# The last weight pieces cut into 100 and 28 rows, and the small loads moved to GpSimd's queue, in a decode step of window attention with a gated MLP

## The chip, the cores and the metric

The kernel runs on one core of one Trainium2 chip. The metric is the device time of one launch in microseconds (us), the median of several runs; lower is better.

## The reference, cut to what matters

```python
def reference(A_x, A_k_cache, A_v_cache, A_wq, A_wo, B_x, B_w_in, B_w_sp, B_b_sp, B_w_out):
    x = A_x                                   # (2, 1, 512): batch 2, one new position
    xn = _layernorm(x, axis=-1)
    # attention over the last 4096 of 32768 cached positions; 32 query heads, 8 kv heads, Dh 128
    q = (xn @ wq)                             # wq (512, 4096)
    scores = einsum("bhqd,bhkd->bhqk", q, k) * Dh ** -0.5
    s = (softmax(scores) @ v) @ wo            # wo (4096, 512)
    # gated MLP
    z = gelu(xn @ w_in)                       # w_in (512, 1792)
    z1, z2 = z[..., :896], layernorm(z[..., 896:])
    y = (z1 * (w_sp * z2 + b_sp)) @ w_out     # w_sp (1, 1), b_sp (1,), w_out (896, 512)
    return x + s * silu(y)
```

Everything is float32. The windows of the two caches are 33.6 MB each, the four weight matrices together some 22 MB, and all of it is read once. The small inputs are `x` (4 KB) and the two scalars `w_sp` and `b_sp`.

## The kernel before

All large loads go through SyncE's DMA queue, in the order in which the program lists them: `win`, `wout`, two halves of `wq`, then the key and value tiles of the eight kv heads, and at last `wo`. Each is one DMA of 128 partition rows. The large tiles except `wout` rotate through a ring of four slots (`slot`, `RING = 4`); a load waits on SyncE until the slot's last reader is done. A cache tile has 4 MB, 32 KB for each of 128 rows.

The work on the engines is one stream per engine, kept in program order by the wrapper `InOrder` (`pe`, `dve`, `act`, `sp`). GpSimd is called directly (`nc.gpsimd`): its memsets, the making of `ident`, and one DMA.

The small loads are the copy of `x` for the layer norm (`xs`, 2 rows of 2 KB, line 91), the scalars `w_sp` and `b_sp` (`wb1`, lines 105 and 106), all three issued by ScalarE, and a second copy of `x` laid out for the final sum (`x4`, line 110), issued by GpSimd. `xs` starts a chain on VectorE (`st`, `mv`, `va`, `rs`, `xn`) that ends in `xnT`, which the first product (`z`, lines 219 to 225) multiplies with `win`. `wb1` is used by one small matmul (`wb_ps`) after it. Then come the queries (`queries(0)` to `queries(3)`), which need `wq`.

For each kv head VectorE turns the key tile (`turn`), TensorE multiplies it with the queries (`scores`), a softmax follows, and TensorE multiplies with the value tile (`values`).

The end, lines 493 to 549, is where most of the change sits. The rows of `wo` belong to three sets of kv heads, `SETS = ((0, 4, 16), (4, 2, 8), (6, 2, 8))`: heads 0 to 3 with 16 columns j, heads 4 and 5 with 8, heads 6 and 7 with 8. They are loaded in pieces, all on 128 rows, a piece of n columns having n * 2 KB in each row. Before the change there are eight pieces: 8 and 8 columns (set 0), 4 and 4 (set 1), and 4, 2, 1 and 1 (set 2). In set 2 they arrive last and in this order. `blocks` lists the pieces. `wo_early(n)` multiplies piece n into the bank `part`; four groups of 32 PSUM rows take turns, and `EARLY = 24` columns, sets 0 and 1, go there. ScalarE copies `part` to `parts`, four matmuls with `rowm` add up its groups into `so`, and the pieces of set 2 are multiplied into `so` directly, four matmuls to a column. VectorE then multiplies `so` with `gate`, adds `x4`, and ScalarE's queue stores the result.

Of the kernel before, what the change touches and what calls it, by code (L numbers as in the profile page):

```python
# [14 lines left out]
P = 128  # L15
# [27 lines left out]
def kernel(  # L43
# [13 lines left out]
    nc = tc.nc  # L57
    pe, dve, act, sp = (InOrder(tc, e) for e in (nc.tensor, nc.vector, nc.scalar, nc.sync))
# [24 lines left out]
    def slot(name, *shape):  # L83
        return ring.tile([P, *shape], F32, tag="slot", name=name)
# [3 lines left out]


    xs = sb.tile([B, D], F32, tag="p", name="xs", bufs=1)  # L90
    act.dma_start(xs, x[:, 0, :])
    win_v = w_in.rearrange("(p k) f -> p k f", p=P)
    win = slot("win", KT, F)
    sp.dma_start(win, win_v)
# [4 lines left out]
    for a in range(0, KT, 2):  # L99
        t = slot(f"wq{a}", 2, HQ * DH)  # L100
# [1 line left out]
        wqt += [t[:, 0], t[:, 1]]  # L102

    wb1 = cst.tile([1, 2], F32, tag="wb1", name="wb1")
    act.dma_start(wb1[:, 0:1], bass.AP(tensor=w_sp.tensor, offset=w_sp.offset, ap=[[1, 1], [1, 1]]))
    act.dma_start(wb1[:, 1:2], bass.AP(tensor=b_sp.tensor, offset=b_sp.offset, ap=[[1, 1], [1, 1]]))
    x4 = cst.tile([P, DC], F32, tag="x4", name="x4")
    nc.gpsimd.memset(x4, 0.0)
    by_group = [[DC, G], [D, B], [1, DC]]
# [351 lines left out]
    def spread_after(p):  # L461
        if p is not None and p.n in ends:
            spread(ends[p.n])
# [26 lines left out]
        scores(cur, 0, 1, 2, 3)  # L490


    wo_s = []
    for kv, n, nj in SETS:
        r0, r1 = kv * REP * DH, (kv + n) * REP * DH
        wo_s.append(wo[r0:r1, :].rearrange("(p j) d -> p j d", j=nj))
    blocks = []
    for first, of in ((0, (0,)), (1, (1, 2))):
        t = slot(f"wo{first}", 16, D)
        a = 0  # L500
        for i in of:
            nj = SETS[i][2]
            for j, n in (((0, 8), (8, 8)), ((0, 4), (4, 4)), ((0, 4), (4, 2), (6, 1), (7, 1)))[i]:
                sp.dma_start(t[:, a : a + n, :], wo_s[i][:, j : j + n, :])
                blocks.append((t[:, a : a + n, :], sets[f"oT{i}"][1], j))
                a += n
    EARLY = 24
# [2 lines left out]
    def wo_early(n):  # L510
        nonlocal done
        t, oT, j = blocks[n]
        for a in range(t.shape[1]):
            g = done % G
            pe.matmul(
                part[32 * g : 32 * g + 32, :], oT[:, j + a, :], t[:, a, :], start=(done < G), stop=(done >= EARLY - G)
            )
            done += 1
# [9 lines left out]
    wo_early(0)  # L528
    gathered(units[-1])
    spread_after(units[-1])  # L530
    for n in range(1, 4):
        wo_early(n)
    parts = sb.tile([P, D], F32, tag="o", name="parts", bufs=1)
    act.activation(parts, part, AF.Copy)
    so = bank("so", DC)
    for g in range(G):
        pe.matmul(so[32 * g : 32 * g + 32, :], rowm, parts[:, g * DC : (g + 1) * DC], start=True, stop=False)
    for n in range(4, len(blocks)):
        t, oT, j = blocks[n]
        for a in range(t.shape[1]):  # L540
            for g in range(G):
                pe.matmul(
                    so[32 * g : 32 * g + 32, :], oT[:, j + a, :], t[:, a, g * DC : (g + 1) * DC],
                    start=False, stop=(j + a == oT.shape[1] - 1),
                )
# [32 lines left out]
```

## Time and profile before

| what | value |
|---|---|
| median of 3 runs | 218.35 us (218.16 to 218.53) |
| the profiled execution | 218.31 us |
| its span, first to last instruction | 216.1 us |
| read from HBM | 89.40 MB, 414 GB/s over the span |
| busy: TensorE, VectorE, ScalarE, GpSimd | 135.0, 104.9, 24.0, 4.0 us |

The profiled execution is 2.2 us longer than its span; that is what lies before the first and behind the last instruction. "Busy" is the time in which an engine executes; none of the four is busy for the whole span. The DMA engines, of which the core has 16, are listed apart, as a share of the 16 that is busy in each stretch of the span. A DMA queue's row gives packets: a transfer of 128 rows has one packet a row and a few small ones that report its end.

### The profile page before, as it was taken

Reading aid. Unit: us, or ns where it says so; the run is one execution under the profiler, and the core shown is the slowest. Engines: PE = TensorE matmul, PEld = TensorE weight load, DVE = VectorE, ACT = ScalarE, POOL = GpSimd, SP = SyncE. Lnnn points to the kernel's source line nnn. Section 1 sums busy time; section 2 is a strip of 40 time slices with the busy share of each in tenths; the row PEclk is TensorE's granted clock in tenths of the full one; section 3 lists DMA queues with packets and bytes.
Section 4 is the critical chain, followed back from the end, with each engine's and each line's share of the span. In section 5 each row is a group of like instructions: output and inputs, shape, how many; then the busy total and the mean of one; then the engine's idle time right before and its main releaser. Section 6 shows DMA issues by size and latency. Waiting matters only on the chain.

```text
span 216.1 us, 2106 instructions
## 1 busy us (share of the span) xinstructions
PE 135.0 (62%) x862; PEld 42.8 (20%) x862; DVE 104.9 (49%) x161; ACT 24.0 (11%) x60; POOL 4.0 (2%) x20
## 2 busy tenths in 40 slices
PE   0173294627774993973594199179567489968653
PEld 0120021113111221320131023033111122342221
DVE  2604014439539539658508910885784684511201
ACT  4103003200001021101021002012000012031010
POOL 7000000000000000000000000000000000000000
PEclk9998569995588598796589559959966969999998
DMA  7999999999999999999999999999999999999990
GB/s 255 425 437 455 418 455 418 429 431 418 455 400 461 403 455 418 443 425 425 443 421 443 406 449 425 449 425 428 437 418 449 400 456 409 443 409 417 417 373 25
DMA packets 4092, 89.52 MB, mean 414 GB/s; under 512 B 486, under 2 KB 498, under 8 KB 884
## 3 DMA queue, kind: packets, MB, share of 16 engines
q1 hardware_dynamic: 4032, 89.39, 96.7%
q8 instruction: 6, 0.10, 0.2%
q14 instruction: 2, 0.02, 0.0%
q10 hardware_dynamic: 20, 0.01, 0.0%
q0 software_dynamic: 32, 0.00, 0.0%
HBM read 89.40 MB, written 0.00 MB: 414 GB/s over the span
## 4 chain that ended last, share of the span: by engine, by line
DMA 71%; PE 13%; DVE 12%; SPq 1%; ACT 1%; issue 1%; ACTq 0%; DVEq 0%
DMA v<-in_A_v_cache_dram 42%; DMA k<-in_A_k_cache_dram 20%; DMA wo<-in_A_wo_dram 9%; DVE kt L37 8%; PE acc L37 7%; PE s L37 3%; PE pp L37 2%; SPq L37 1%; ACT p L37 1%; DVE pT L37 1%; DVE sm L37 1%; DVE qw L37 1%; DVE both L37 0%; PE col L37 0%; DVE res L37 0%
## 5 line engine op out<-in xcount | busy, mean ns | idle before, releaser
L37 DVE STREAM_TRANSPOSE kt<-k 128x2048 f32<-128x2048 f32 x32 | 72.5, 2286 | 3.5 <-DMA k<-in_A_k_cache_dram 3.5
L37 PE MATMUL acc<-v,pT 128*32 128x512 f32 x256 | 40.1, 781 | 11.4 <-DMA v<-in_A_v_cache_dram 10.5
L37 PE MATMUL s<-kt,qw 128*32 128x512 f32 x256 | 39.8, 669 | 4.6 <-DVE kt L37 4.1
L37 PE MATMUL pp<-p,swap 128*128 128x512 f32 x16 | 12.4, 871 | 21.3 <-ACT p L37 21.3
L37 DVE CUSTOM_DVE_ANT_1 sm<-s,own 128x512 f32<-128x512 f32 x8 | 5.5, 692 | 34.2 <-PE s L37 34.2
L37 PEld LDWEIGHTS acc<-v,pT 128*32 128x32 f32 x256 | 10.5, 152 | 39.4 <-issue 35.6
L37 PE MATMUL q_ps<-wq,xnT 128*32 128x512 f32 x64 | 9.7, 732 | 11.0 <-DMA wq<-in_A_wq_dram 11.0
L37 ACT ACTIVATE o<-acc,diag 128x128 f32<-128x128 f32 x30 | 8.7, 369 | 69.3 <-PE acc L37 68.9
L37 PEld LDWEIGHTS s<-kt,qw 128*32 128x32 f32 x256 | 9.5, 120 | 34.0 <-issue 20.8
L37 ACT ACTIVATE p<-sm,nb 128x512 f32<-128x512 f32 x8 | 5.8, 725 | 70.8 <-DVE nb L37 70.8
L37 DVE TENSOR_TENSOR lsum<-pl,diag 128x4 f32<-128x4 f32 x3 | 0.5, 162 | 16.7 <-PE pl L37 16.7
L37 DVE STREAM_TRANSPOSE pT<-pp 128x512 f32<-128x512 f32 x8 | 5.7, 714 | 5.7 <-PE pp L37 5.6
L37 PE MATMUL z<-win,xnT 128*32 128x448 f32 x32 | 5.7, 887 | 3.9 <-DMA win<-in_B_w_in_dram 3.9
L37 PE MATMUL part<-wo,oT 128*32 128x512 f32 x48 | 6.0, 600 | 2.8 <-DMA wo<-in_A_wo_dram 2.8
L37 PE MATMUL col<-o,selw 128*32 128x128 f32 (+1 forms) x28 | 7.6, 436 | 0.0
L37 PEld LDWEIGHTS pp<-p,swap 128*128 128x128 f32 x16 | 2.8, 218 | 22.0 <-ACT p L37 22.0
L37 PE MATMUL mo<-mg,same 128*128 128x16 f32 x16 | 3.2, 273 | 5.8 <-DVE mg L37 5.3
L37 DVE TENSOR_TENSOR res<-so,gate 128x128 f32<-128x128 f32 x1 | 0.3, 292 | 10.4 <-PE so L37 10.4
L37 ACT ACT_TABLE_LOAD x4 | 5.1, 1283 | 2.0 <-issue 1.9
L37 PE MATMUL xnT_ps<-ident,xn 2*128 2x2 f32 x4 | 0.6, 252 | 7.5 <-DVE xn L37 7.5
L37 PE MATMUL qj_ps<-qT,selj 128*128 128x64 f32 x8 | 2.0, 428 | 4.9 <-DVE qT L37 4.9
L37 PEld LDWEIGHTS q_ps<-wq,xnT 128*32 128x32 f32 x64 | 2.0, 126 | 14.6 <-DMA wq<-in_A_wq_dram 11.1
(110 smaller groups left out, 65.0 us busy)
## 6 DMA issues: line engine op xcount, KB each, us to landing
k<-in_A_k_cache_dram SPq DMA_DIRECT2D x8, 4096.0 KB, 23.4
v<-in_A_v_cache_dram SPq DMA_DIRECT2D x8, 4096.0 KB, 31.2
wq<-in_A_wq_dram SPq DMA_DIRECT2D x2, 4096.0 KB, 28.9
wo<-in_A_wo_dram SPq DMA_DIRECT2D x2, 2048.0 KB
win<-in_B_w_in_dram SPq DMA_DIRECT2D x1, 3584.0 KB, 11.1
wo<-in_A_wo_dram SPq DMA_DIRECT2D x3, 1024.0 KB, 23.2
wout<-in_B_w_out_dram SPq DMA_DIRECT2D x1, 1792.0 KB, 15.0
wo<-in_A_wo_dram SPq DMA_DIRECT2D x1, 512.0 KB, 26.9
```

Of the source, the lines that this page charges most:

```text
L37: return self.tc.keep_in_program_order(call(*args, **kwargs))
```

## The change

Three edits. `xs`, `w_sp` and `b_sp` are issued on GpSimd's queue instead of ScalarE's, ahead of `x4`. The second piece of set 1, 4 columns, becomes two pieces of 2 columns; the loop over `wo_early` goes one piece further for it, so that the same 24 columns go into `part`. And each of the last two pieces of set 2, 1 column each (256 KB), is loaded by two DMAs, one for rows 0 to 99 and one for rows 100 to 127. The matmuls are the same in number and shape.

```diff
-    act.dma_start(xs, x[:, 0, :])
+    nc.gpsimd.dma_start(xs, x[:, 0, :])
...
-    act.dma_start(wb1[:, 0:1], bass.AP(tensor=w_sp.tensor, offset=w_sp.offset, ap=[[1, 1], [1, 1]]))
-    act.dma_start(wb1[:, 1:2], bass.AP(tensor=b_sp.tensor, offset=b_sp.offset, ap=[[1, 1], [1, 1]]))
+    nc.gpsimd.dma_start(wb1[:, 0:1], bass.AP(tensor=w_sp.tensor, offset=w_sp.offset, ap=[[1, 1], [1, 1]]))
+    nc.gpsimd.dma_start(wb1[:, 1:2], bass.AP(tensor=b_sp.tensor, offset=b_sp.offset, ap=[[1, 1], [1, 1]]))
...
+    LATE = ((2, 6), (2, 7))
...
-            for j, n in (((0, 8), (8, 8)), ((0, 4), (4, 4)), ((0, 4), (4, 2), (6, 1), (7, 1)))[i]:
-                sp.dma_start(t[:, a : a + n, :], wo_s[i][:, j : j + n, :])
+            for j, n in (((0, 8), (8, 8)), ((0, 4), (4, 2), (6, 2)), ((0, 4), (4, 2), (6, 1), (7, 1)))[i]:
+                deal = ((0, 100), (100, P)) if (i, j) in LATE else ((0, P),)
+                for p0, p1 in deal:
+                    sp.dma_start(t[p0:p1, a : a + n, :], wo_s[i][p0:p1, j : j + n, :])
                 blocks.append((t[:, a : a + n, :], sets[f"oT{i}"][1], j))
                 a += n
...
-    for n in range(1, 4):
+    for n in range(1, 5):
         wo_early(n)
...
-    for n in range(4, len(blocks)):
+    for n in range(5, len(blocks)):
```

## The prediction, made before the changed kernel ran

> **What bounds the kernel now.** I read the page's slices first, then its DMA queues, then the chain that ended last, and last the timeline and the windows of the final stretch.
>
> ```profile
> DMA  7999999999999999999999999999999999999990
> q1 hardware_dynamic: 4032, 89.39, 96.7%
> q8 instruction: 6, 0.10, 0.2%
> q14 instruction: 2, 0.02, 0.0%
> q10 hardware_dynamic: 20, 0.01, 0.0%
> q0 software_dynamic: 32, 0.00, 0.0%
> DMA 71%; PE 13%; DVE 12%; SPq 1%; ACT 1%; issue 1%; ACTq 0%; DVEq 0%
> ```
>
> The DMA engines are at 90% or more in every slice but the first and the last. So the waits of the middle cost nothing as long as the queue stays fed, and time can be lost or won only where the transfers start, where they end, or if fewer than 16 engines work. The end is told by the chain of waits:
>
> ```profile
> 164.31 28.21 DMA v<-in_A_v_cache_dram
> 192.53 19.79 DMA wo<-in_A_wo_dram
> 212.33 0.04 issue
> 212.37 0.47 PE so L37 x8
> ```
>
> The kernel ends with the last piece of wo, which lands at 192.53 + 19.79 = 212.32; then come only eight matmul instructions, two VectorE operations and the store. The timeline shows the pieces ahead of it, each waited for in its turn:
>
> ```profile
> 207.33 1.06 PE L37 MATMUL part<-wo,oT 128*32 128x512 f32 x8 [1.43 <-DMA wo<-in_A_wo_dram]
> 208.46 0.60 ACT L37 ACTIVATE parts<-part 128x512 f32<-128x512 f32 x1 [10.35 <-PE part L37]
> 209.11 0.43 PE L37 MATMUL so<-parts,rowm 128*32 128x128 f32 x8 [0.72 <-ACT parts L37]
> 209.91 2.25 PE L37 MATMUL so<-wo,oT 128*32 128x128 f32 x56 [0.38 <-DMA wo<-in_A_wo_dram]
> 211.07 0.38 PEld L37 LDWEIGHTS so<-wo,oT 128*32 128x32 f32 x16 [0.35 <-DMA wo<-in_A_wo_dram]
> 211.73 0.16 PEld L37 LDWEIGHTS so<-wo,oT 128*32 128x32 f32 x8 [0.28 <-DMA wo<-in_A_wo_dram]
> 212.37 0.43 PE L37 MATMUL so<-wo,oT 128*32 128x128 f32 x8 [0.21 <-DMA wo<-in_A_wo_dram]
> ```
>
> Set 2's four pieces start at 209.91, 211.07, 211.73 and 212.37. One column (256 KB) thus takes 212.37 - 211.73 = 0.64 us. Now the windows of the last stretch; the last two columns are the busy share of the 16 DMA engines and GB/s:
>
> ```profile
> 209.70:209.90 0.20, 0.00 (x0) 0.02 (x1) 0.00 (x0) 0.00 (x0) 0.00 (x0) 1.00 0.94 358
> 209.90:210.10 0.20, 0.18 (x8) 0.20 (x12) 0.00 (x0) 0.00 (x0) 0.00 (x0) 1.00 0.68 266
> 210.10:210.30 0.20, 0.20 (x16) 0.20 (x12) 0.00 (x0) 0.00 (x0) 0.00 (x0) 1.00 0.57 215
> 210.70:210.90 0.20, 0.20 (x12) 0.03 (x3) 0.00 (x0) 0.00 (x0) 0.00 (x0) 1.00 0.55 205
> 210.90:211.10 0.20, 0.12 (x8) 0.03 (x4) 0.00 (x0) 0.00 (x0) 0.00 (x0) 1.00 0.41 154
> 211.10:211.30 0.20, 0.20 (x8) 0.20 (x12) 0.00 (x0) 0.00 (x0) 0.00 (x0) 1.00 0.43 164
> 211.30:211.50 0.20, 0.20 (x16) 0.15 (x8) 0.00 (x0) 0.00 (x0) 0.00 (x0) 1.00 0.30 113
> 211.50:211.70 0.20, 0.20 (x9) 0.00 (x0) 0.00 (x0) 0.00 (x0) 0.00 (x0) 1.00 0.14 51
> 211.70:211.90 0.20, 0.18 (x11) 0.16 (x8) 0.00 (x0) 0.00 (x0) 0.00 (x0) 1.00 0.03 10
> ```
>
> This is the view that decides. The 16 engines do not finish together. About half of them have nothing left from 210.1 on (0.57 of 16 is 9, and 205 GB/s is half of what all of them moved). Of the rest two stop near 210.95, and six, one after the other, between 211.1 and 211.8. Every large transfer gives each engine the same 8 rows (4032 packets are 28 transfers of 128 rows and 16 reports), so the late half must have lost time to something else. The queues offer it: six packets of 0.10 MB together, some 16 KB each, and two smaller ones, all of instructions. Eight fetches, eight late engines: I take it that each fetch held up one engine and that nothing later makes it up.
>
> **The last two pieces, 100 and 28 rows.** What matters is how the rows are dealt. The 20 packets of q10 are the four small transfers of ScalarE's queue: 2 + 1 + 1 + 8 rows are 12, so 8 report an end, where a transfer of 128 rows has 16 reports. That fits equal shares on as many engines as the first dimension allows: 2 for xs, 1 for each scalar, 4 for the store, which is laid out as 4 by 2. By equal shares 100 rows go to ten engines, 10 rows each, and 28 rows to fourteen, 2 rows each. If both start at the same end of the numbering, then for each of the two pieces ten engines carry 12 rows instead of 8, four carry 2, and two carry none. A row costs 0.64 / 8 = 0.08 us on its engine. Over both pieces that is +8 rows, +0.64 us, for ten engines; -12 rows, -0.96 us, for four; -16 rows, -1.28 us, for two.
>
> [...]
>
> The end is then set by the last engine of the ten. No view says which numbers the late engines have. If the very last one, done at about 211.8, is among the ten, the end comes 0.64 us later. That is the value that I take: ten places of sixteen hold it if nothing is known, and for a gain all six of the latest would have to be the six spared ones. Bounds: below, -0.2 us, worked out with the first rival; above, +1.0 us, if the ten engines, writing blocks of ten rows at once, get in each other's way by a quarter of their 24 rows (24 x 0.08 = 1.92 us, a quarter is 0.5, half of it hidden by the earlier ends of the others). The matmuls of these pieces each wait for two transfers instead of one; behind them on TensorE is only the next piece.
>
> **The second piece of set 1 in two.** The piece of 4 columns is worked on at 207.33; the copy and the fold of part are over at 209.11 + 0.43 = 209.54, and only at 209.91, after 0.38 us of waiting for data, does the next product start. An earlier half would be done earlier and wait longer: no gain. Its price is one more packet a row. Set 2's piece of 2 columns took 211.73 - 211.07 = 0.66 to the next start and 1.16 from the one before; twice 1.25 for two such pieces against the 2.49 us between the starts of 4-column pieces (204.84 to 207.33) is 0.01 us. I take 0.02, between 0 and 0.05. If the cover of 0.38 us were gone, the fold would start set 2's products late, yet these have another 0.1 to 0.3 us of slack at each piece.
>
> ```profile
> 204.84 1.06 PE L37 MATMUL part<-wo,oT 128*32 128x512 f32 x8 [0.56 <-DMA wo<-in_A_wo_dram]
> 180.67 12.20 SPq L37 DMA_DIRECT2D wo<-in_A_wo_dram  x8
> ```
>
> SyncE has three more DMAs to issue (one here, two for the cut pieces). The eight of now took 12.20 us with their waits for the slot, so three more take 4.6 us at the most; the last was issued at 192.53 and landed 19.79 us later, and that lead covers them. Nothing is queued behind them on SyncE but the end; without the lead, their issue would stand in full ahead of the last landing.
>
> **The small loads on GpSimd.**
>
> ```profile
> 0.75 0.56 ACTq L37 DMA_DIRECT2D xs<-in_A_x_dram  x1
> 1.30 0.68 POOL L110 DMA_DIRECT2D x<-in_A_x_dram  x1 [0.21 <-POOL ident masks.py:197]
> x<-in_A_x_dram POOLq DMA_DIRECT2D x1, 4.0 KB, 6.5
> 3.28 0.68 DVE L37 BATCH_NORM_STATS2 st<-xs 2x6 f32<-2x512 f32 x1 [0.50 <-DMA xs<-in_A_x_dram]
> 8.24 0.17 DVE L37 COPY xnT<-xnT_ps 128x8 f32<-128x8 f32 x1 [0.87 <-PE xnT_ps L37]
> 11.99 5.70 PE L37 MATMUL z<-win,xnT 128*32 128x448 f32 x32 [3.86 <-DMA win<-in_B_w_in_dram]
> PE q_ps L37 <- DMA wq<-in_A_wq_dram: 11.0, 2, 7.9
> ```
>
> Now xs is there at 3.28. On GpSimd's queue it takes what x takes, 0.68 us of issue and 6.5 us to land, at worst until about 8, at best as quickly as now. From st to the end of xnT are 8.41 - 3.28 = 5.1 us, so xnT comes between 8.4 and 13.1, and z, which waits for win until 11.99, starts 0 to 1.1 us late. This is covered: the first queries wait up to 7.9 us for wq afterwards. If that cover were gone, it would cost the 1.1 us. SyncE's load of the second key tile waits for z's slot, and with a queue in which a landing comes 19.79 or 28.21 us after its issue (the two of the chain above), 1 us later is nothing. GpSimd's own work behind the three issues, the making of ident and the memsets, comes some 3 x 0.68 = 2 us later; rowm (VectorE) waits for ident, and st behind it waits for xs longer than that. The scalars are needed only after z. ScalarE is rid of issuing, 0.56 us for xs, that nobody waited for. I take 0, between -0.1 (two engines start the large transfers without xs in between) and +0.1 (more small packets on all engines).
>
> **Sum.** Against the profiled execution's 218.31: +0.64 + 0.02 + 0 gives 218.97; the median of the runs is 0.04 above this execution, so 219.0 us. The measurement of this kernel tells about 0.2% (0.44 us) from no change.
>
> **Rivals.** First, not slower: the six latest engines are exactly the six spared ones. For it speaks the count, six of six, with a shift (0.64 + 0.96 or 1.28) about as large as their lag of some 1.2 to 1.7 us behind the half that is done at 209.9 to 210.1; against it, that nothing ties them to these numbers. The two engines done near 210.95 must then be among the ten, and end at 210.95 + 0.64 = 211.6 instead of 211.8: -0.2 us, 218.15 with the rest. TensorE would allow it: the 2-column piece still lands for 211.07, its 16 weight loads took 0.38 us, those of the two last pieces would take as long, and all is over well before 212.84, where it is now. This decides from the point where no engine done after 211.1 is among the ten; one at 211.2 would make it a draw.
>
> Second: the shares are not equal, the rows are dealt over all 16 engines as evenly as they go (7 and 2). Then an engine has at most 9 rows for 8 in each piece, and the end is 2 x 0.08 = 0.16 us later: 218.5. Against it speak the 20 packets of q10. [...]
>
> Third: the last engine is among the spared ones but a middle one of the six is not. The end is then 0.64 us behind 211.3 to 211.6, so at 211.94 to 212.24 where it is now 211.8: 218.5 to 218.8.
>
> **How the numbers follow.** My forecast gets 0.47, with its own range of 218.8 to 219.3; the first rival 0.33, the second 0.08, the third 0.12. Slower by over 0.2%: 0.47 and a little of the third, less the forecast's own lower edge, 0.48. Faster by over 0.2% needs 0.44 us, twice what the first rival gives; 0.09 for a fetch that moves or a start that gains more than I see. The rest, 0.43, is within 0.2%. The range of 217.9 to 219.3 takes in the first rival with its spread and the forecast.
>
> **What would show it.** The page's q1 row would count 27 x 144 + 2 x (128 + 10 + 14) = 4192 packets by equal shares, 4208 if every transfer used 16. In the timeline the last two starts would be near 212.1 and 213.0 instead of 211.73 and 212.37, 0.8 to 0.96 us apart, while the pieces before them keep their times. The windows would show a share near 0.6 until the end instead of a fall in steps. st would start later than 3.28, z up to 1.1 us later, and the first queries when they do now. I am wrong if the last piece lands before 212.3, or if the large transfers themselves end the stretch before wo at another time.

## The result, and the profile after

The changed kernel takes 220.25 us (median of 6 runs, 219.59 to 221.09) where the one before takes 218.44 (6 runs, 217.71 to 219.09): a ratio of 1.0084, 95% interval 1.0058 to 1.0110, so 1.8 us slower. The forecast was 219.0 in a range of 217.9 to 219.3: right in its direction, and about a third of the size. The profiled execution took 220.89 us, its span is 218.1, 2.0 us more than before.

The rows of the page on the DMA queues and the end of the chain of waits, after:

```profile
q1 hardware_dynamic: 4192, 89.39, 96.4%
q0 software_dynamic: 128, 0.01, 0.0%
q10 hardware_dynamic: 12, 0.00, 0.0%
204.77 9.38 DMA wo<-in_A_wo_dram
214.28 0.46 PE so L37 x8
```

q1 has exactly the 4192 packets that equal shares on ten and fourteen engines give. The 12 packets of q10, which now has the store alone, are its 8 rows and 4 reports, as the prediction counted them. The end is still the last piece of wo: its product starts at 214.28 instead of 212.37, which is 1.91 of the 2.0 us by which the span grew. The timeline of the end, after:

```profile
204.80 5.34 PE L37 MATMUL part<-wo,oT 128*32 128x512 f32 x32
211.09 1.06 PE L37 MATMUL so<-wo,oT 128*32 128x128 f32 x32
212.42 0.65 PE L37 MATMUL so<-wo,oT 128*32 128x128 f32 x16 [0.27 <-DMA wo<-in_A_wo_dram]
213.32 0.43 PE L37 MATMUL so<-wo,oT 128*32 128x128 f32 x8 [0.25 <-DMA wo<-in_A_wo_dram]
214.28 0.43 PE L37 MATMUL so<-wo,oT 128*32 128x128 f32 x8 [0.53 <-DMA wo<-in_A_wo_dram]
```

The loss has two parts. The piece of 2 columns, which is not split and lies ahead of the split ones in the queue, starts at 212.42 instead of 211.07: 1.35 us. From there to the last start are 1.86 us instead of 1.30: 0.56 us. TensorE was late as well in this execution (part took 5.34 us for its last 32 matmul instructions, with a granted clock of 0.50 from 205 to 208), but each of the last three products still waits for data, so that is not what ended it. The windows show where the 1.35 us went (the last two columns are the share of the DMA engines and GB/s):

```profile
208.50:209.00 0.50, 0.50 (x8) 0.13 (x4) 0.00 (x0) 0.00 (x0) 0.00 (x0) 1.00 1.03 410
209.00:209.50 0.50, 0.50 (x8) 0.13 (x4) 0.00 (x0) 0.00 (x0) 0.00 (x0) 1.00 0.99 270
209.50:210.00 0.50, 0.50 (x8) 0.00 (x0) 0.00 (x0) 0.00 (x0) 0.00 (x0) 1.00 0.99 246
210.50:211.00 0.50, 0.15 (x7) 0.15 (x11) 0.00 (x0) 0.30 (x1) 0.00 (x0) 1.00 1.02 221
211.50:212.00 0.50, 0.50 (x24) 0.38 (x16) 0.00 (x0) 0.00 (x0) 0.00 (x0) 1.00 0.52 119
212.50:213.00 0.50, 0.50 (x16) 0.30 (x16) 0.00 (x0) 0.00 (x0) 0.00 (x0) 1.00 0.11 41
213.00:213.50 0.50, 0.25 (x12) 0.19 (x8) 0.00 (x0) 0.00 (x0) 0.00 (x0) 1.00 0.06 25
```

Four of the same windows before the change:

```profile
209.00:209.50 0.50, 0.39 (x8) 0.16 (x8) 0.00 (x0) 0.06 (x1) 0.00 (x0) 1.00 1.06 410
210.00:210.50 0.50, 0.50 (x23) 0.50 (x25) 0.00 (x0) 0.00 (x0) 0.00 (x0) 1.00 0.56 213
210.50:211.00 0.50, 0.50 (x20) 0.23 (x10) 0.00 (x0) 0.00 (x0) 0.00 (x0) 1.00 0.51 193
211.00:211.50 0.50, 0.42 (x16) 0.38 (x16) 0.00 (x0) 0.00 (x0) 0.00 (x0) 1.00 0.38 143
```

From 209 to 211 all 16 engines are busy after the change, and together they move 221 to 270 GB/s instead of 410. Before the change the rate fell too, but the share fell with it (0.56 and 213 GB/s). All of them busy at a little over half the rate: I read this as engines that held each other up here. The trace's single packets show it row by row: a row of 4 KB, which can only belong to a piece that is not split, takes 0.26 us in the mean between 209 and 211 instead of 0.16, and a row of 2 KB 0.14 instead of 0.086. From 212.5 on, when one or two engines are left, rows of 2 KB take 0.085 us again. The last row of 4 KB ends 0.96 us later than before; the remaining 0.39 of the 1.35 us lies between this row and the start of its product, and was not traced.

### The profile page after: what moved, and what is told of

It is laid out like the page before. It is cut to its first block, busy times and chain, and to the rows that moved or that the text cites. A ratio compares the mean times of both kernels' runs of the same rounds, so it can differ in the third digit from the quotient of the medians.

```text
span 218.1 us, 2113 instructions
## 1 busy us (share of the span) xinstructions
PE 139.2 (64%) x862; PEld 44.8 (21%) x862; DVE 104.9 (48%) x161; ACT 24.0 (11%) x60; POOL 5.7 (3%) x23
## 3 DMA queue, kind: packets, MB, share of 16 engines
q1 hardware_dynamic: 4192, 89.39, 96.4%
## 4 chain that ended last, share of the span: by engine, by line
DMA 63%; PE 16%; DVE 15%; SPq 1%; ACT 1%; issue 1%; ACTq 0%; DVEq 0%
DMA v<-in_A_v_cache_dram 28%; DMA k<-in_A_k_cache_dram 20%; DMA wo<-in_A_wo_dram 15%; DVE kt L37 11%; PE acc L37 7%; PE s L37 6%; PE pp L37 3%; SPq L37 1%; ACT p L37 1%; DVE pT L37 1%; DVE sm L37 1%; DVE qw L37 1%; PE col L37 0%; DVE both L37 0%; DVE mg L37 0%
## 5 line engine op out<-in xcount | busy, mean ns | idle before, releaser
L37 PE MATMUL acc<-v,pT 128*32 128x512 f32 x256 | 41.9, 813 | 11.4 <-DMA v<-in_A_v_cache_dram 10.5
L37 PE MATMUL pp<-p,swap 128*128 128x512 f32 x16 | 13.1, 915 | 21.2 <-ACT p L37 21.2
L37 PEld LDWEIGHTS acc<-v,pT 128*32 128x32 f32 x256 | 10.8, 155 | 40.8 <-issue 37.0
L37 PE MATMUL part<-wo,oT 128*32 128x512 f32 x48 | 7.2, 750 | 0.0
```

The costliest lines, as they stand in the source:

```text
L37: return self.tc.keep_in_program_order(call(*args, **kwargs))
```

## The experiments

My theory after the result, drawn from the slow rows above: many engines that write neighbouring rows at a time, as in a load of 100, 28 or 64 of the 128 rows, slow each other, and in a load of all 128 they do not. The rivals are that the loss is the uneven count of rows, or the number of small transfers, or the reads from memory, or one of the other two edits. Ratios are to the kernel before, run beside on the same chip.

### One edit alone, and halves instead of 100 and 28

The 100/28 split alone:

```diff
+                deal = ((0, 100), (100, P)) if (i, j) in LATE else ((0, P),)
```

> Only the 100/28 split of the last two pieces; small loads and set 1 as before. My theory now: the whole loss of about 1.8 us is this edit's, 0.64 us by the uneven rows and the rest because the engines move rows at some 205 GB/s instead of 360 while the split pieces are under way; so 1.5 to 2.1 us slower than before, with the same slow 2 KB rows in the windows of the end. Rival: half of the loss comes from the other two edits (a later start, a later last sum); then 0.6 to 1.0 us slower, and the windows of the end at full rate until the early half is done.

Measured: 220.07 us, ratio 1.0088 (1.0064 to 1.0113). By the medians that is 1.9 us, as much as the three edits together. The profile agrees: the piece of 2 columns starts at 212.42 as in the changed kernel, the last piece at 214.08.

```profile
212.42 1.21 PE L37 MATMUL so<-wo,oT 128*32 128x128 f32 x24 [1.06 <-DMA wo<-in_A_wo_dram]
214.08 0.42 PE L37 MATMUL so<-wo,oT 128*32 128x128 f32 x8 [0.44 <-DMA wo<-in_A_wo_dram]
```

The small loads alone (`nc.gpsimd.dma_start` for xs and the two scalars):

> Only the three small loads on GpSimd's queue. My theory: z starts about 0.9 us late as in the changed kernel (12.85 for 11.99), and everything from the first queries on stands where it did: within 0.2 us of before. Rival that the loss is a late start: 0.5 us slower or more, with the first key tile's landing moved by as much.

Measured: 218.37 us, ratio 1.0015 (0.9998 to 1.0032). z starts at 12.78 instead of 11.99, and the first queries at 25.9, where they start before the change.

Set 1's second piece in two (`(0, 4), (4, 2), (6, 2)`), alone:

> Only set 1's second piece in two. My theory: no change, within 0.2 us; the windows of the end as in before, half the engines done near 210. Rival: the last sum is late (in the changed kernel part ended at 210.15 instead of 208.4) because of this edit, and 0.3 us or more are lost.

Measured: 218.25 us, ratio 0.9997 (0.9983 to 1.0012): nothing. It is at the same time a control: a piece cut by columns, with twice the packets.

Equal halves of rows for the last two pieces:

```diff
+                deal = ((0, 64), (64, 128)) if (i, j) in LATE else ((0, P),)
```

> The last two pieces split into rows 0 to 63 and 64 to 127, so that equal shares give each of the 16 engines 4 + 4 rows, as many as before. Theory that uneven rows alone cost time: no change, within 0.2 us. Theory that engines which write rows of one half of the partitions at the same time get in each other's way: rows take 0.13 to 0.17 us instead of 0.085, the two pieces up to twice their 1.3 us, and the end is 0.5 to 1.3 us later.

Measured: 219.71 us, ratio 1.0075 (1.0051 to 1.0098), though by equal shares every engine has as many rows as before (q1 counts 4064 packets: the 4032 of before and 16 reports for each of the two added transfers). The 1.5 us of the medians (219.71 against 218.21) are more than the 0.5 to 1.3 expected. In the profiled execution, at 219.36 the shortest of its six, the weights of the piece of 2 columns are loaded at 212.19 instead of 211.07 and those of the last piece at 213.35 instead of 212.37. Its windows, and these two lines:

```profile
208.50:209.00 0.50, 0.50 (x8) 0.13 (x4) 0.00 (x0) 0.00 (x0) 0.00 (x0) 1.00 1.03 377
209.00:209.50 0.50, 0.50 (x8) 0.13 (x4) 0.00 (x0) 0.00 (x0) 0.00 (x0) 1.00 1.07 254
210.00:210.50 0.50, 0.18 (x4) 0.00 (x0) 0.00 (x0) 0.25 (x1) 0.00 (x0) 1.00 0.90 193
212.19 0.38 PEld L37 LDWEIGHTS so<-wo,oT 128*32 128x32 f32 x16 [0.27 <-DMA wo<-in_A_wo_dram]
213.35 0.16 PEld L37 LDWEIGHTS so<-wo,oT 128*32 128x32 f32 x8 [0.39 <-DMA wo<-in_A_wo_dram]
```

The same fall at a share of 0.9 and more. The uneven count alone is therefore not the main cost.

### Small transfers, or reads

The same pieces cut by columns, twice 128 rows of 1 KB:

```diff
+                cuts = ((0, D // 2), (D // 2, D)) if (i, j) in LATE else ((0, D),)
+                for c0, c1 in cuts:
+                    sp.dma_start(t[:, a : a + n, c0:c1], wo_s[i][:, j : j + n, c0:c1])
```

> Before, with each of the last two pieces loaded in two DMAs that halve the columns (128 rows of 1 KB each) instead of the rows. As many DMAs at the same place as the split by rows. Theory that neighbouring rows at one time are what slows: within 0.2 us of before, full rate until half the engines are done near 210. Theory that small DMAs at the end cost by their number: 1 us slower or more, like the halves by rows.

Measured: 218.43 us, ratio 1.0013 (0.9994 to 1.0032), about 0.3 us at the median, which the interval does not tell from nothing. In its windows the full rate holds until half of the engines are done:

```profile
209.00:209.50 0.50, 0.28 (x8) 0.01 (x1) 0.00 (x0) 0.00 (x0) 0.00 (x0) 1.00 1.01 373
209.50:210.00 0.50, 0.33 (x13) 0.36 (x17) 0.00 (x0) 0.00 (x0) 0.00 (x0) 1.00 1.02 361
```

So the number of transfers and the size of their rows do not explain a loss of 1.5 to 1.9 us. The 100/28 split with other source rows:

```diff
+    near = wo[HQ * DH - 2 * P :, :].rearrange("(p j) d -> p j d", j=2)
...
+                    from_ = wo_s[i][p0:p1, j : j + n, :] if (i, j) not in LATE else near[p0:p1, j % 2 : j % 2 + 1, :]
+                    sp.dma_start(t[p0:p1, a : a + n, :], from_)
```

> As the 100/28 split alone, but the two pieces are read from rows of wo that lie 4 KB apart in memory instead of 16 KB (other weights than the reference's, so this part of the sum is another one); the destination rows are the same. Theory that the rows' place in the on-chip memory slows them: as the split alone, 1.5 to 2.1 us slower than before, rows of 0.13 to 0.16 us. Theory that the reads from memory slow each other: rows back near 0.085 us and 0.6 us slower than before, as the row count gives.

Measured: 220.16 us, ratio 1.0086 (1.0053 to 1.0119), as the split alone. Source rows four times closer together make no difference, so their spacing is not the cause.

### The same cut on a large transfer

If neighbouring rows are what slows, the cost must grow with the bytes; how it goes with the number of rows is to be seen. The second half of wq, 128 rows of 32 KB, was loaded in 2, 4 and 8 DMAs, each engine having, by equal shares, the same 8 rows in all (q1 counts 4048, 4080 and 4144 packets, 16 more for each added DMA, which are its reports):

```diff
+        step = 64 if a == 2 else P        # 32 and 16 in the other two
+        for p0 in range(0, P, step):
+            sp.dma_start(t[p0 : p0 + step], wq_v[p0 : p0 + step, a : a + 2, :])
```

> Before, with the second half of wq (128 rows of 32 KB, 4 MB, 9.7 us of the queue's time) loaded in two DMAs of 64 rows, 4 rows to each engine in each; nothing else changed. [...] Theory that more and smaller DMAs cost a fixed time each: under 0.5 us slower. Theory that only late, small rows are affected: no change.

> The same in four DMAs of 32 rows, 2 rows to each engine in each. [...] If the rate goes with the number of rows, a quarter of it: some 25 to 29 us slower. A fixed time for each DMA: three times what the halves lose.

> The same in eight DMAs of 16 rows, one row to each engine in each. [...]

Measured: 229.56 us (ratio 1.0524, 1.0487 to 1.0560) with 64 rows, 229.24 (1.0500, 1.0470 to 1.0529) with 32, 243.23 (1.1138, 1.1101 to 1.1174) with 16; the kernel before took 217.99 beside them. That is +11.6, +11.3 and +25.2 us for a transfer of 9.7 us (4.19 MB at some 430 GB/s). One window of each, in the order before, 64, 32 and 16 rows:

```profile
26.00:30.00 4.00, 4.00 (x18) 1.01 (x18) 0.00 (x0) 0.00 (x0) 0.00 (x0) 0.50 1.12 483
```

```profile
26.00:30.00 4.00, 3.20 (x16) 0.60 (x16) 0.00 (x0) 0.00 (x0) 0.00 (x0) 0.50 1.00 205
```

```profile
26.00:30.00 4.00, 3.64 (x17) 0.67 (x17) 0.00 (x0) 0.00 (x0) 0.00 (x0) 0.50 1.09 221
```

```profile
26.00:30.00 4.00, 2.13 (x12) 0.60 (x16) 0.00 (x0) 0.00 (x0) 0.00 (x0) 0.50 0.98 123
```

At the same full share 205, 221 and 123 GB/s: half, half, and a bit over a quarter. (These rates are rough, since packets straddle the windows; the 483 of before is high for this reason, over its whole span it moves 414.) The single packets are sharper: a row of 32 KB takes 1.21 us before, 2.56 with 64 rows, 2.57 with 32 and 4.22 with 16, which is 2.1, 2.1 and 3.5 times as long. With 8 rows on each engine that is 10.8, 10.9 and 24.1 us, nearly all of the three losses. The pages agree: q1's time, its share of 16 engines over the span (96.7% of 216.1 us before, 96.8% of 227.4, 96.9% of 227.0, 97.0% of 241.8), grows by some 178, 176 and 409 us, of which these rows give 173, 174 and 385. Two and four transfers cost the same, so it is not a price for each transfer; 64 and 32 rows cost the same and 16 twice that. Why it goes so with the number of rows, these runs do not show. The cut narrows the source as well as the destination; a large load with its reads alone changed was not run, so against the memory side speak only the small pieces above.

### How many engines are late, and which

Three quarters of the matmuls of scores and values left out, so that TensorE fetches fewer instructions (`for j in range(1)` in `scores`, `n = 1` in `values`):

> Before, with three quarters of the matmuls of scores and values left out (768 of TensorE's 1724 instructions; the softmax and what follows work on other numbers); every load stays. Theory that each fetch of TensorE's instructions holds up one DMA engine for good: three 16 KB fetches instead of six in the span, and near 210.3 to 210.9 some five or six engines at work instead of eight (a share of 0.33 to 0.4 for 0.53 to 0.55); the end as before within 0.3 us, since one early fetch is enough for one late engine. Rival that the late half has another cause: the share as before.

Measured: 218.66 us, ratio 1.0008 (0.9984 to 1.0032). Its fetches and windows:

```profile
q8 instruction: 3, 0.05, 0.1%
q14 instruction: 2, 0.02, 0.0%
```

```profile
210.00:210.50 0.50, 0.50 (x20) 0.28 (x12) 0.00 (x0) 0.00 (x0) 0.00 (x0) 1.00 0.43 160
210.50:211.00 0.50, 0.39 (x15) 0.34 (x16) 0.00 (x0) 0.00 (x0) 0.00 (x0) 1.00 0.24 90
211.00:211.50 0.50, 0.50 (x20) 0.19 (x12) 0.00 (x0) 0.00 (x0) 0.00 (x0) 1.00 0.16 61
```

Five fetches instead of eight, and a share of 0.24 instead of 0.51 between 210.5 and 211, of 16 engines: about four late instead of eight, fewer than the five or six expected. Between 211 and 211.5 it is 0.16 instead of 0.38, some three engines instead of six, with three fetches of 16 KB instead of six. This is one kernel, and TensorE's work differs as well, but the number of late engines falls with the fetches. The end cannot be told from before, as expected; the reason given there, that one early fetch is enough for one late engine, was my estimate.

More rows for the same ten engines, ahead of the last two pieces, first as seven DMAs of 10 rows into the tile of w_out:

```diff
+                if (i, j) == (2, 6):
+                    for m in range(FT):
+                        sp.dma_start(wout[0:120:12, m, :], pairs[10 * m : 10 * m + 10, 0, :])
```

> Before, with seven more DMAs ahead of the last two pieces, each of 10 rows of 2 KB that lie 12 partitions apart (into a tile that is no longer read). By equal shares the same ten engines get 7 more rows each, but the ten rows of one DMA lie far apart in the partitions. Theory that the last engine is one of the ten: 7 x 0.08 = 0.56 us and a little for seven reports, so 0.6 to 0.9 us slower. Rival that the last engine is one of the six others, and all of the changed kernel's loss is slow rows: under 0.2 us. If rows 12 apart slow each other as well: over 1.2 us.

Measured: 220.89 us, ratio 1.0113 (1.0084 to 1.0141), and it says nothing of the question. SyncE's timeline shows why:

```profile
184.56 26.19 SPq L37 DMA_DIRECT2D wout<-in_A_wo_dram  x7
211.34 0.81 SPq L37 DMA_DIRECT2D wo<-in_A_wo_dram  x2
```

The seven DMAs write one tile, and from 180 us on SyncE waited six times for a DMA, 14.3 us in total, so the last two pieces were issued only at 211.34, and the queue ran dry (a share of 0.05 from 211 to 211.5). Then as two DMAs of 10 rows of 8 KB, each into a tile of its own:

```diff
+                    for m in range(2):
+                        spare = sb.tile([P, 4, D], F32, tag="kt", name=f"spare{m}", bufs=4)
+                        sp.dma_start(spare[0:120:12], wo_s[2][10 * m : 10 * m + 10, 0:4, :])
```

> Before, with two more DMAs ahead of the last two pieces, each of 10 rows of 8 KB that go 12 partitions apart into tiles that are no longer read; nothing waits for them. The run with seven such DMAs told nothing of this, since they waited for each other on SyncE. By equal shares the same ten engines get two rows of 8 KB more (0.31 us each, 0.62 us), the others nothing. Theory that the last engine is one of the ten: 0.6 to 0.8 us slower. Rival that it is one of the other six: under 0.2 us. If rows 12 apart slow each other as neighbouring ones do: 1 us or more.

Measured: 219.72 us against 218.56 beside it, ratio 1.0068 (1.0044 to 1.0093), 1.2 us by the medians and 1.5 by the ratio. Its windows have 295, 238 and 266 GB/s at a share of 1.13, 1.01 and 1.13 between 209 and 210.5, and a row of 4 KB takes 0.27 us in the mean instead of 0.16. So rows 12 apart slow things as well while the other engines are still on 128-row pieces, which is the third of the cases expected. Why they do is not shown. This run does not separate the count of rows from the slower rows.

## Why the prediction was wrong, point by point

**What bounds the kernel: right.** The last landing still ends the chain, and the 1.91 us at the last start are nearly all of the kernel's loss.

**How the rows are dealt: right.** 4192 packets, and the last two starts 0.96 us apart (213.32 and 214.28), which is 12 rows of 0.08 us. An engine with 2 rows or none would have needed 0.16 us or nothing, so the engine that ends last is one of the ten. The prediction gave this ten places of sixteen, so that it came out so was in part luck. The first rival, in which the six latest are spared, does not fit: its end would have been the earlier one. The third also ends on one of the ten, 0.14 to 0.44 us later than before; the 0.56 us below are nearer to the forecast's 0.64, but the slow rows blur this, and no view tells the engines apart. One sign was wrong: the share was to stay near 0.6 until the end, and it fell in steps, to 0.52, 0.11 and 0.06.

**The uneven rows: right in size.** 0.64 us was forecast; the stretch from the piece of 2 columns to the last piece grew by 0.56 us.

**The failed step** is the sentence that the pieces before the split ones "keep their times", and with it the upper bound. I did see that ten engines writing blocks of ten rows might get in each other's way, but priced it at a quarter of their own 24 rows, half of it hidden, some 0.25 us net (0.64 + 0.25 is 0.89; the bound says 1.0), and left it out of the value that I took. The measured term is 1.35 us, and it falls on the piece ahead: the half of the engines that is done early starts on the split rows near 209, and the late half, which sets the end and is still on the piece of 2 columns, then moves its own rows more slowly: 0.26 us for a row of 4 KB instead of 0.16, with all engines together at 221 to 270 GB/s instead of 410. The halves, where the count term is zero, show this term alone: 1.5 us by the medians, 1.12 us at the piece of 2 columns in the profiled execution. The sum took the early engines' time as free; in the changed kernel it was not, since their work slowed the late ones. Of the 1.91 us at the last start the sum had a term for 0.56 us (it said 0.64) and none for 1.35.

**The second rival fell.** 4192 packets are equal shares, not rows dealt over all 16 engines, and its end would have been 0.16 us later where the last product starts 1.91 us later. Nor is a cut free where the shares are equal: halves lose 1.5 us on two pieces of 256 KB and 11.6 us on 4 MB.

**Set 1's piece in two: right as far as it can be told.** 0.02 us was forecast, and a ratio of 0.9997 (0.9983 to 1.0012) measured, which does not resolve so small a term.

**The small loads: right.** They cost nothing that can be told, and the steps came as worked out: in the profile after, st starts at 7.67 and z at 12.85, within the 0 to 1.1 us allowed, and it is covered, as the first key tile's landing shows (2.79 + 43.96 = 46.75, before 3.02 + 43.78 = 46.80).

```profile
7.67 0.68 DVE L37 BATCH_NORM_STATS2 st<-xs 2x6 f32<-2x512 f32 x1 [2.76 <-DMA xs<-in_A_x_dram]
12.85 5.33 PE L37 MATMUL z<-win,xnT 128*32 128x448 f32 x32 [0.34 <-DVE xnT L37]
2.79 43.96 DMA k<-in_A_k_cache_dram
```

**The fetches behind the late half** were argued before, and the run with fewer of TensorE's instructions bears them out in the main: about four late engines for five fetches, where eight had eight.

No run beat the kernel before: what the experiments teach is to leave the transfers at 128 rows, and that is what it has.

## What to carry to other kernels

Load tiles on all 128 partition rows and, where pieces are wanted, cut them by columns: here pieces cut so cost nothing that can be told (ratios of 0.9997 and 1.0013), while a cut by rows moved the same bytes at a little under half the rate with 64 or 32 rows, and at 0.29 of it with 16, even when every engine had the same work. In these runs, windows with all DMA engines busy at half the usual GB/s (205 at a share of 1.00 with 64 rows of wq) meant that they held each other up; half the engines busy at half the GB/s (213 at a share of 0.56 before the change) meant that the others were merely done early, and only the second was spare time. Even that was not free to fill in the changed kernel: an engine still at work then took 0.26 us for a row of 4 KB instead of 0.16.

## What the runs showed of the hardware

About half of the DMA engines ended late: in the span of 216 us before the change two ended about 1 us behind the others and six between 1.1 and 1.8 us, and the number went with the fetches of instructions (about eight late for eight fetches, some four for five), no more than 0.2% of the DMA engines' time. That each fetch holds up one engine for good, as the prediction took it, fits this and was not seen directly. A fetch of 16 KB took an engine 1.0 to 1.1 us in the trace and one of 8 KB 0.3 us, less than most of these delays; where the rest comes from is open.

What I had not expected: the store held ScalarE's queue longer where it was its only DMA, 1.15 us once the small loads have moved and 0.64 us before (the line of ScalarE's queue in the timeline after):

```profile
215.42 1.15 ACTq L37 DMA_DIRECT2D out_dram<-res  x1
```

It is the same with the small loads alone (1.15 us), and 0.63 to 0.65 us in the runs that leave them on ScalarE. Why was not tried. What it costs lies within that kernel's ratio of 1.0015 (0.9998 to 1.0032).
